# The last two passes of an attention and feed-forward kernel put in order by a planner, and h by w_out in seven block products instead of eight

## The chip, the cores and the metric

The kernel runs on one core of a Trainium2 chip. The metric is the device time of one execution in microseconds; the profile and the trace come from one profiled execution of the same program. In them PE is the matrix engine, PEld its weight loads, DVE the vector engine, ACT the scalar engine, POOL GpSimd and SP the engine that issues most of the DMAs; L1012 is line 1012 of the kernel before.

## The reference

```python
# q, k, v: (8, 8, 576, 64), block-causal attention in blocks of 64
scores = scale * np.matmul(q, k.transpose(0, 1, 3, 2))        # masked where block_i < block_j
attn = np.exp(scores - max);  attn = attn / (sum + 1e-09)
x = np.matmul(attn, v).transpose(0, 2, 1, 3).reshape(4608, 512)
a = x @ w_a            # (512, 1536)
b = x @ w_b            # (512, 1536)
out = (a * b) @ w_out  # (1536, 512)
```

## The kernel before, in words

Every product of the second half is made in float32 quality from three fast products: an operand is cut into a high part (`hi`, a cast by ACT) and a low part (`lo`, what is left, a subtraction by DVE or POOL), and PE adds `hi*hi`, `hi*lo` and `lo*hi`. So one block product of depth 128 is three matmuls.

The 1536 columns of `w_a` and `w_b` are twelve blocks `f` of 128. `f` 0 to 3 are done together with the attention, in the first 598 us: attention and the first feed-forward blocks are a list of operations (`Op`), each with an engine, a cost from the table `TOOK` and a due time (`key`), and `plan()` walks through time and, on the engine that is free first, takes the ready operation with the lowest `key`. The instructions are then issued in that order under `tc.manual_schedule`. The first pass writes its share of the output to a DRAM tensor `part`.

`f` 4 to 7 (`ps_` 0, the second pass) and `f` 8 to 11 (`ps_` 1, the third) are the last passes. Each goes over six pairs of tiles (`tt`, NT2 = 6) of 2 x 384 columns of x. In a pair each `f` is a unit (`pair_unit`): a and b of both tiles come from seven block products instead of eight for each of two depth blocks (`kp`, KP = 2): Y, X1, W1, V1, X2, W2, V2. That is 7 x 2 x 3 = 42 matmuls a unit, L1012, 168 a pair. The operands are sums and differences of blocks of x (`sums_x`, L977 to L993: four subtractions into `xt` and `xr`, four casts into `xh`, four subtractions into `xl` for each `kp`) and of the weights (`sums`). The results need sums too: a unit has four PSUM banks (y, x, w, v). ACT copies y into SBUF (`u`, L1029), DVE adds x (L1030), and five more DVE additions with w, v and u (L1032 to L1039), of which some only wait for the last products W2 and V2, give the factors; two DVE products give `h` of both tiles, and each is cut into hi and lo (`split`, L130 and L133). That makes nine DVE and three ACT instructions a unit. No engine but PE writes a bank.

After the four units `pair_out` makes h by `w_out` for the pair: eight outputs (`j`, `o`), each 4 f x 3 matmuls, 96 a pair, L1058. In the second pass ACT copies each output to `pt` and a GpSimd DMA adds it to `part` (L1122). In the third pass SP loads what `part` holds (L1116), DVE adds (L1124), and SP stores to `outT` (L1125).

The order in the last passes is that of the code, with each engine's queue put in order by the scheduler; `behind_of` holds some DVE instructions back behind others. The weights arrive as float64 and are converted (`convert_w`) by ACT and DVE in the background of these passes: a generator that `background(...)` advances by a step every so many matmuls (`STEP1`, `STEP2`). The second pass's weights are kept in SBUF; those of the third are staged through DRAM (`wabd`, `wod`) and loaded back when the second pass ends. The tiles of x for the next pair (`xr`, L967) are loaded by SP one pair ahead, and `sums_x` for the next pair stands in the code behind unit 2.

Of the kernel before, what the change touches and what calls it, by code (L numbers as in the profile page):

```python
# [17 lines left out]
P = 128  # L18
# [48 lines left out]
STEP1 = 1150  # L67
STEP2 = 2950
# [4 lines left out]
def attention_then_bilinear_ffn(  # L73
# [6 lines left out]

    wo: bass.AP,
    outT: bass.AP,
# [7 lines left out]
    wab, wo = wab.bitcast(I32), wo.bitcast(I32)  # L90
# [14 lines left out]
    part = dram.tile([DO, T], F32, name="part")  # L105
    wabd = dram.tile([F2, KP, P, 2 * NW * P], F32, name="wabd")
    wod = dram.tile([F2, P, 2 * DO], F32, name="wod")
# [80 lines left out]
    wopool = pool(ctx, "wopool", F1)  # L188
# [4 lines left out]

    def new_wo(f):
        w_sb[f][1] = wopool.tile([P, 2, DO], F32R, tag="wo", name=f"wo{f}")
# [21 lines left out]
    def convert_w(todo, lo_eng, paced=False, stage=None, raw=None):  # L217
# [6 lines left out]
        for k, (f, i) in enumerate(todo):  # L224
            now, raw = raw, ahead(*todo[k + 1]) if k + 1 < len(todo) else None
            xf, spare = yield from convert(now, f"w{f}_{i}", paced, own and k == 0)
            if stage:
                st = stage.tile([P, 2, NW if i < KP else NO, P], F32R, tag="st", name=f"st{f}_{i}")
            if i == KP:
                if not stage and w_sb[f][1] is None:  # L230
                    new_wo(f)
                o = st.rearrange("p j c n -> p j (c n)") if stage else w_sb[f][1]
                split(o[:, 0], o[:, 1], xf, nc.scalar, lo_eng)
            elif f < F1:
                ab = w_sb[f][0]
                hi, lo = (ab[:, j, i].rearrange("p c n -> p (c n)") for j in range(2))
                split(hi, lo, xf, nc.scalar, lo_eng)
            else:
                ab = st if stage else w_sb[f][0][:, i]
                yield from sums(ab[:, 0], ab[:, 1], xf, spare, paced)  # L240
            if stage:
                f -= F1 + F2
                nc.sync.dma_start(wod[f] if i == KP else wabd[f, i], f32(st).rearrange("p j c n -> p (j c n)"))
            yield
# [45 lines left out]
    w1 = pool(left, "w1", 1)  # L290
    for f in range(F1):
        w_sb[f] = [w1.tile([P, 2, KP, 4, P], F32R, name=f"wab{f}"), None]
        new_wo(f)
# [68 lines left out]
    def plan():  # L362
# [567 lines left out]
    def start_conv2():  # L930
        raw = fetch(wab[F1, :, 0], f"w{F1}_0")
        box["g"] = convert_w(parts(range(F1, F1 + F2)), nc.vector, paced=True, raw=raw)
# [13 lines left out]
    n_bank = 0  # L946

    def bank(nm):
        nonlocal n_bank
        n_bank += 1  # L950
        return (ps_mm if n_bank % 8 < MM else ps_more).tile([P, 512], F32, tag="mm", name=nm)


    w2 = pool(right, "w2", F2, "right", reuse_waits="tile")
    rpool = pool(right, "rpool", 2 * KP, "right", reuse_waits="tile")
    tpool = pool(right, "tpool", 2, "right", reuse_waits="tile")
    upool = pool(right, "upool", 2, "right", reuse_waits="tile")
# [4 lines left out]
    def load_x(tt):  # L962

        raw = []
        for cc in range(NCC):
            raw.append(rpool.tile([P, 2, T2], F32, tag="xr", name=f"xr{cc}_{tt}"))
            nc.sync.dma_start(  # L967
                raw[cc].rearrange("p j n -> p (j n)"), xd[cc * P:(cc + 1) * P, 2 * tt * T2:2 * (tt + 1) * T2])
        return raw

    def sums_x(raw, kp, nm):

        hi = xk.tile([P, NW, T2], F32R, tag="xh", name=f"xh_{nm}_{kp}", bufs=3)
        t = tpool.tile([P, 3, T2], F32, tag="xt", name=f"xt_{nm}_{kp}")
        a, b = raw[2 * kp:2 * kp + 2]
        v = nc.vector
        for ins in (v.tensor_tensor(t[:, 1], b[:, 1], a[:, 1], op=ALU.subtract),  # L977
                    v.tensor_tensor(a[:, 1], a[:, 1], a[:, 0], op=ALU.subtract)):
            if nm[0] == "0" and nm != "0_0":
                behind_of(ins, "hf")  # L980
        v.tensor_tensor(t[:, 0], b[:, 1], a[:, 1], op=ALU.subtract)
        nc.scalar.copy(hi[:, 0:2], a)
        nc.scalar.copy(hi[:, 2:4], t[:, :2])
        v.tensor_tensor(t[:, 2], b[:, 0], t[:, 0], op=ALU.subtract)
        nc.scalar.copy(hi[:, 4:6], b)
        nc.scalar.copy(hi[:, 6], t[:, 2])
        yield
        lo = xk.tile([P, NW, T2], F32R, tag="xl", name=f"xl_{nm}_{kp}", bufs=2)
        for ins in (
                v.tensor_tensor(lo[:, 0:2], a, f32(hi[:, 0:2]), op=ALU.subtract),  # L990
                v.tensor_tensor(lo[:, 2:4], t[:, :2], f32(hi[:, 2:4]), op=ALU.subtract),
                v.tensor_tensor(lo[:, 4:6], b, f32(hi[:, 4:6]), op=ALU.subtract),
                v.tensor_tensor(lo[:, 6], t[:, 2], f32(hi[:, 6]), op=ALU.subtract)):  # L993
            if nm[0] == "0" and nm != "0_0":
                behind_of(ins, "hf")
        yield hi, lo

    Y, X1, W1, V1, X2, W2, V2 = (4, 2), (0, 0), (3, 1), (5, 3), (1, 4), (6, 5), (2, 6)  # L1000

    def pair_unit(f, xs, nm, hs, halves):

        w = w_sb[f][0]
        y, x, w_, v_ = (bank(f"ps{i}_{nm}")[:, :T2] for i in "yxwv")

        def prod(ps, what, start, kps=range(KP)):
            iw, ix = what
            for kp in kps:
                (xh, xl), wt = xs[kp], w[:, kp]  # L1010
                for i, j in ((0, xh), (0, xl), (1, xh)):
                    nc.tensor.matmul(  # L1012
                        ps, wt[:, i, iw], j[:, ix], start=start and kp == 0 and i == 0 and j is xh,
                        stop=kp == KP - 1 and i == 1, skip_group_check=not start)
                    yield

        if halves:
            for ps, what, kp in ((y, Y, 0), (x, X1, 0), (w_, W1, 0), (y, Y, 1), (x, X1, 1), (v_, V1, 0),
                                 (w_, W1, 1), (v_, V1, 1)):
                yield from prod(ps, what, True, [kp])  # L1020
        else:
            for ps, what in ((y, Y), (x, X1), (w_, W1), (v_, V1)):
                yield from prod(ps, what, True)
        k = (f - F1) % F2
        (ha, la), (hb, lb) = (
            [h_tile(int(4 * k + 2 * j + i >= 10), T2, F32R, f"h{i}_{nm}_{j}") for i in range(2)] for j in range(2))
        u, t, c = (upool.tile([P, T2], F32, tag=f"u{i}", name=f"u{i}_{nm}", bufs=2 - i // 2) for i in range(3))
        v = nc.vector
        nc.scalar.copy(u, y)  # L1029
        v.tensor_tensor(u, x, u, op=ALU.add)  # L1030
# [6 lines left out]
        v.tensor_tensor(t, c, t, op=ALU.mult)  # L1037
        split(hb, lb, t, nc.scalar, nc.vector)
        v.tensor_tensor(u, v_, u, op=ALU.add)  # L1039
        last["hf"] = v.tensor_tensor(u, x, u, op=ALU.mult)  # L1040
        last["la"] = split(ha, la, u, nc.scalar, nc.vector)
        hs[f] = (ha, la), (hb, lb)

    def pair_out(fs, hs, nm, out):

        todo = [(j, o) for j in (1, 0) for o in range(NO)]
        n = {}

        def run(j, o, fs_):
            k = j, o  # L1050
            if k not in n:
                n[k] = 0, bank(f"pso{j}_{o}_{nm}")[:, :T2]
            i, ps = n[k]
            osl = slice(o * P, (o + 1) * P)
            for f in fs_:
                (hh, hl), wt = hs[f][j], w_sb[f][1]
                for a, b in ((0, hh), (0, hl), (1, hh)):
                    nc.tensor.matmul(ps, wt[:, a, osl], b, start=i == 0, stop=i == 3 * len(fs) - 1)  # L1058
                    i += 1
                    yield  # L1060
            n[k] = i, ps
            if i == 3 * len(fs):
                out(j, o, ps)

        for k in todo[:2]:
            yield from run(*k, fs[:-1])
        for k in todo[:2]:
            yield from run(*k, fs[-1:])
        for k in todo[2:]:
            yield from run(*k, fs)  # L1070
# [136 lines left out]
```

## Time and profile before

| what | value |
|---|---|
| median of three runs | 1162.55 us (1158.05 to 1163.65) |
| the profiled execution's own time | 1162.46 us |
| its span in the trace (first to last instruction) | 1160.5 us |
| last passes, first matmul to last | 598.5 us to 1156.9 us |
| matmuls in the last passes | 3168 (12 pairs x 264) |

A page of the profile lists busy time of each engine, the chain of work that ended last, and groups of instructions by line. A row of the windows view gives busy times in a stretch of the span, with the granted clock of PE (1.00 is full speed). In the trace an instruction's duration is printed in microseconds (timeline, chain) or as a mean in nanoseconds (groups). "[1.17 <-DVE u_z]" behind a row says how long its engine stood idle before it and what ended that. Some per cent of the matmul records are missing from the trace, so counts there run a few short.

### The profile page before, as it was taken

How to read it: one execution, taken by the hardware profiler on the slowest of the kernel's cores; microseconds unless marked ns; L12 is line 12 of the kernel's file. 1: busy time of each engine (PE TensorE's matmuls, PEld its weight loads, DVE VectorE, ACT ScalarE, POOL GpSimd, SP SyncE). 2: the span in 40 equal slices, each digit the busy share in tenths (PEclk: the TensorE clock that was granted, in tenths of full speed). 3: DMA queues.
4: the chain of work that ended last, by engine and by line, in shares of the span. 5: the costliest groups of instructions: out<-in, count | busy, mean ns of one | idle time of the engine just before them, and what ended most of it. 6: DMA issues, size and time to landing. Idle time of an engine off the chain costs nothing.

```text
span 1160.5 us, 23135 instructions
## 1 busy us (share of the span) xinstructions
PE 1114.2 (96%) x8400; PEld 1045.4 (90%) x8400; DVE 865.7 (75%) x1813; ACT 539.9 (47%) x1422; POOL 369.5 (32%) x553
## 2 busy tenths in 40 slices
PE   6887989999999999998999999999999999999998
PEld 3566878889988899898999999999999999999998
DVE  5889867778767777752899888797786767767754
ACT  4876556566656656642464453343443221312210
POOL 4686656566656565551100220210201000000000
PEclk8999999999999999998999999999999999999999
DMA  4545787888777777776252662744788415325032
GB/s 160 160 160 150 188 229 225 217 218 219 216 194 211 221 202 223 203 194 177 82 162 73 175 163 81 177 115 126 173 296 225 137 36 156 85 79 163 1 110 69
DMA packets 85554, 187.14 MB, mean 161 GB/s; under 512 B 14272, under 2 KB 40896, under 8 KB 85440
## 3 DMA queue, kind: packets, MB, share of 16 engines
q1 hardware_dynamic: 78528, 176.21, 51.7%
q0 software_dynamic: 6912, 9.44, 5.1%
q8 instruction: 67, 1.10, 0.4%
q14 instruction: 47, 0.39, 0.1%
HBM read 87.03 MB, written 47.19 MB: 116 GB/s over the span
## 4 chain that ended last, share of the span: by engine, by line
PE 74%; DVE 7%; ACT 6%; DMA 5%; SPq 3%; POOL 3%; issue 2%; ACTq 0%; DVEq 0%; POOLq 0%
PE pso_z L1058 16%; PE ps L254 10%; PE psx_z L1012 9%; PE psw_z L1012 9%; PE psv_z L1012 9%; PE pso L254 6%; PE av L660 5%; PE psy_z L1012 4%; PE x L506 3%; ACT e L552 3%; SPq L651 3%; DVE nm L525 2%; PE y L506 2%; DMA qr<-qT 1%; POOL e L595 1%
## 5 line engine op out<-in xcount | busy, mean ns | idle before, releaser
L254 PE MATMUL ps<-xh,wab 128*128 128x288 f32 x1024 | 212.9, 298 | 0.0
L1058 PE MATMUL pso_z<-h_z,wo 128*128 128x384 f32 x1152 | 203.3, 334 | 0.0
L1058 PEld LDWEIGHTS pso_z<-h_z,wo 128*128 128x128 f32 x1152 | 199.9, 188 | 0.4 <-ACT h_z L130 0.3
L254 PEld LDWEIGHTS ps<-xh,wab 128*128 128x128 f32 x1024 | 166.2, 189 | 5.7 <-issue 4.8
L595 POOL TENSOR_SCALAR e<-e,rc 128x512 f32<-128x512 f32 (+3 forms) x256 | 150.6, 607 | 45.3 <-DVE rc L586 45.3
L254 PE MATMUL ps<-xl,wab 128*128 128x288 f32 x512 | 153.9, 301 | 0.6 <-POOL xl L703 0.6
L1122 POOL DMA_DIRECT2D part<-pt x48 | 42.9, 1055 | 283.1 <-ACT pt L1121 275.2
L130 ACT CAST h_z<-u_z 128x384 fp32r<-128x384 f32 x96 | 49.3, 513 | 176.1 <-DVE u_z L1037 160.0
L600 DVE STREAM_TRANSPOSE bl<-e 128x512 f32<-128x512 f32 (+1 forms) x224 | 119.5, 583 | 14.8 <-POOL e L595 10.2
L1012 PE MATMUL psx_z<-xh,wab 128*128 128x384 f32 x384 | 116.0, 338 | 1.2 <-DVE u_z L1030 1.2
L1012 PE MATMUL psv_z<-xh,wab 128*128 128x384 f32 x384 | 116.2, 337 | 0.0
L1012 PE MATMUL psw_z<-xh,wab 128*128 128x384 f32 x384 | 116.1, 338 | 0.0
L660 PE MATMUL av<-at,v 128*64 128x128 f32 (+1 forms) x1920 | 101.3, 264 | 10.4 <-DMA at<-bl 6.4
L660 PEld LDWEIGHTS av<-at,v 128*64 128x64 f32 x1920 | 96.1, 141 | 16.6 <-issue 11.6
L254 PEld LDWEIGHTS ps<-xl,wab 128*128 128x128 f32 x512 | 96.5, 188 | 6.1 <-issue 4.6
L254 PE MATMUL pso<-hh,wo 128*128 128x288 f32 x480 | 101.0, 299 | 0.0
L506 PE MATMUL x<-k,q 64*128 64x512 f32 (+1 forms) x344 | 66.1, 479 | 23.5 <-ACT e L552 17.5
L254 PEld LDWEIGHTS pso<-hh,wo 128*128 128x128 f32 x480 | 78.1, 189 | 5.2 <-issue 4.0
L525 DVE TENSOR_REDUCE nm<-x 128x2 f32<-128x1024 f32 x64 | 73.1, 1142 | 5.7 <-PE x L506 4.7
L760 POOL TENSOR_TENSOR hl<-hf,hh 128x288 fp32r<-128x288 f32 x56 | 46.3, 826 | 97.4 <-ACT hh L756 91.8
L552 ACT ACTIVATE e<-y,nm 128x192 f32<-128x192 f32 (+1 forms) x128 | 62.0, 487 | 26.0 <-DVE nm L525 23.5
L1012 PEld LDWEIGHTS psx_z<-xh,wab 128*128 128x128 f32 x384 | 71.0, 187 | 1.6 <-DVE u_z L1030 1.5
(133 smaller groups left out, 2303.3 us busy)
## 6 DMA issues: line engine op xcount, KB each, us to landing
at<-bl SPq DMA_DIRECT2D x448, 112.0 KB, 2.3
xr<-xd SPq DMA_DIRECT2D x48, 384.0 KB, 4.0
cv<-wab SPq DMA_DIRECT2D x24, 512.0 KB, 4.6
v<-vm SPq DMA_DIRECT2D x32, 320.0 KB, 3.4
xd<-xf SPq DMA_DIRECT2D x32, 288.0 KB, 2.9
part<-ob SPq DMA_DIRECT2D x64, 144.0 KB, 2.1
part<-pt POOLq DMA_DIRECT2D x48, 192.0 KB, 7.0
pt<-part SPq DMA_DIRECT2D x48, 192.0 KB, 3.3
```

The lines of the kernel that those rows point to most:

```text
L130: nc.scalar.copy(hi, src)
L254: nc.tensor.matmul(ps, w_, d_, start=(i == 0), stop=(i == n - 1))
L506: nc.tensor.matmul(out[:, h], qq[r, q0[t]:q0[t] + P], keys, start=j == 0, stop=j == len(qk) - 1)
L525: nc.vector.tensor_reduce(st["nm"][:, :, t], view, axis=AX.X, op=ALU.max, negate=True)
L552: nc.scalar.activation(out, view, AF.Exp, bias=bias, accum_out=sm[:, h, t, :1])
L595: nc.gpsimd.tensor_scalar(ev, ev, st["rc"][:, h, t:t + 1], 1.0, op0=ALU.mult, op1=ALU.mult)
L600: nc.vector.transpose(dst, es[h][t].rearrange("p (c g q) -> p c g q", g=NQ, q=QB))
L660: nc.tensor.matmul(out[d], v[:, h, c], a[:, qs, h, e_], start=start, stop=stop, skip_group_check=True)
L760: nc.gpsimd.tensor_tensor(lo, box2["hf"], f32(hi), op=ALU.subtract)
L1012: nc.tensor.matmul(ps, wt[:, i, iw], j[:, ix], start=start and kp == 0 and i == 0 and j is xh, stop=kp == KP - 1 and i == 1, skip_group_ch ...
L1058: nc.tensor.matmul(ps, wt[:, a, osl], b, start=i == 0, stop=i == 3 * len(fs) - 1)
L1122: nc.gpsimd.dma_start(part[o * P:(o + 1) * P, ts], t, accum_op=ALU.add)
```

## The change

Both last passes become `Op`s as well and go through the planner, with costs for their instructions in `TOOK` (p1 to p4 for 1 to 4 depth blocks on PE, d1, d2 on DVE, a1, a2 on ACT, g1, g2 on POOL, lx for a load of x, acc for an accumulating DMA). The order on PE is that of the code (all products write the name "pe"); for the other engines the planner decides, by due times relative to PE's `clock`. `plan(look)` may now take an operation that becomes ready up to 0.3 us later, if its due time is lower.

A unit now has three banks. W1 and W2 go into the bank of y: ACT copies y to `u`, DVE adds x, and ACT copies the sum back into y's PSUM bank (`middle`, L1100), on which PE then adds W1 (accumulating, not starting) and later W2. Between the two, ACT copies the bank to `t` and DVE adds v (`fourth`). With W2 and V2 the bank holds a factor, and DVE forms `v+u` (`second`). DVE has seven instructions a unit in the second pass instead of nine, ACT five instead of three.

The third pass makes h by `w_out` in seven block products of 8 as well: 28 block products of three matmuls, 84 a pair instead of 96, from sums of blocks of `w_out` (`wq`, four parts, converted and staged like the third pass's `wab`) and differences of h of two units (three more DVE subtractions for every two units, and 14 cuts a pair instead of 8). Its results are made with `middle`, `fourth` and `second` as in a unit. The outputs are added to `outT` by accumulating GpSimd DMAs (`part` is now `outT` itself, so the third pass loads nothing), except in the last pair, where SP loads, DVE adds and SP stores (`finish`); there six `pt` buffers serve eight outputs, and the load for the seventh and eighth is issued behind the store of the first and second.

Of the low parts of x two a pair (`X_POOL`: `kp` 1, groups 0 and 1, 768 columns each) go to POOL instead of DVE. Of the weights for these passes the eight `wab` parts are still converted in the old background; the four parts of `w_out` for f 4 to 7, and all that is staged, are converted by planned operations. Buffers are fixed tiles instead of pools that rotate; `xr` has one set of four.

```diff
-STEP1 = 1150
-STEP2 = 2950
+X_POOL = {(1, 0), (1, 1)}
+BEHIND = 5.0
+LOOK = 0.3
...
-    part = dram.tile([DO, T], F32, name="part")
+    part = outT
...
-            o = min((o for o in ready[e] if since(o) <= t), key=lambda o: (o.key, o.n))
+            o = min((o for o in ready[e] if since(o) <= t + look), key=lambda o: (o.key, o.n))
+            t = max(t, since(o))
...
-        y, x, w_, v_ = (bank(f"ps{i}_{nm}")[:, :T2] for i in "yxwv")
...
-        nc.scalar.copy(u, y)
-        v.tensor_tensor(u, x, u, op=ALU.add)
-        yield from prod(x, X2, False)
-        v.tensor_tensor(t, w_, u, op=ALU.add)
-        yield from prod(w_, W2, False)
-        v.tensor_tensor(t, v_, t, op=ALU.add)
-        yield from prod(v_, V2, False)
-        v.tensor_tensor(c, w_, u, op=ALU.add)
-        v.tensor_tensor(t, c, t, op=ALU.mult)
...
+        def middle(self):
+            self.u = turn_of("u", 4)
+            u, y, x = us[self.u], self.view("y"), self.view("x")
+            name = "u", self.u
+            do("a1", ACT_, lambda: nc.scalar.copy(u, y), [self.name("y")], [name], key=clock[0] - 100)
+            do("d1", DVE_, tt(u, x, u, ALU.add), [self.name("x")], [name], key=clock[0] - 100)
+            do("a1", ACT_, lambda: nc.scalar.copy(y, u), [name], [self.name("y")], key=clock[0] - 100)
+
+        def fourth(self, to, to_name):
+            y = self.view("y")
+            do("a1", ACT_, lambda: nc.scalar.copy(to, y), [self.name("y")], [to_name], key=clock[0] - 100)
+            do("d1", DVE_, tt(to, self.view("v"), to, ALU.add), [self.name("v")], [to_name], key=clock[0] - 100)
...
+        for i in range(F2):
+            if i == 0:
+                units[1].product("Y", ks)
+            units[i].product("X2", ks)
+            units[i].product("W1", ks)
+            fourth(i)
...
+                units[i + 1].middle()
+                units[i + 1].product("V1", ks)
+            else:
+                fill()
+            units[i].product("W2", ks)
+            units[i].product("V2", ks)
+            tail_of(i)
+            if i == 0 and not final:
+                x_load((tt_ + 1) % NT2)
...
+        for z, q in enumerate(outs):
+            q.product("X2", [0])
+            q.product("W1", both_)
+            out(z, q, "fourth")
...
+        do("d1", DVE_, tt(t, src, t, ALU.add), [src_name], [name], key=clock[0] - 50)
+        ts = slice((2 * NT2 - 2 + j) * T2, (2 * NT2 - 1 + j) * T2)
+        do("so", SP_, lambda: nc.sync.dma_start(outT[o * P:(o + 1) * P, ts], t), [name], [], key=clock[0])
+        if z + 6 < len(places):
+            part_load(z + 6)
...
+    for i in range(2 * NT2):
+        tile_pair(*divmod(i, NT2))
+    with tc.manual_schedule(engines={getattr(mybir.EngineType, e) for e in LAGS}):
+        for o in plan(LOOK):
+            o.fn()
```

Where the change moves instructions, the queues of two engines show it. The first place is ACT's queue in units 1 to 3 of a pair of the third pass. Before, ACT has the copy of y (L1029, bank `psy`) and two casts of h (`h0`, L130) for each unit:

```order
L130 CAST h0_z1_4_9_1_13146<-u1_z1_4_9_13149 128x384
L1029 COPY u0_z1_4_10_13225<-psy_z1_4_10_13193 128x384
L130 CAST h0_z1_4_9_0_13144<-u0_z1_4_9_13148 128x384
L130 CAST h0_z1_4_10_1_13223<-u1_z1_4_10_13226 128x384
L1029 COPY u0_z1_4_11_13300<-psy_z1_4_11_13268 128x384
```

Now it has, for each unit, the copy of the bank (L1098), the copy back into it (L1100), the copy for `fourth` (L1104), and more casts of h (`hz`, L1113), with a cast of the next x between them (L1008):

```order
L1113 CAST hz8_0_8536<-u3_8519 128x384
L1104 COPY t0_8520<-bank0_8508 128x384
L1098 COPY u1_8517<-bank3_8511 128x384
L1100 COPY bank3_8511<-u1_8517 128x384
L1008 CAST xh2_8402<-xt1_7883 128x768
L1113 CAST hz2_1_8540<-u3_8519 128x384
L1113 CAST hz4_1_8542<-u0_8516 128x384
L1104 COPY t1_8521<-bank3_8511 128x384
```

What moved: a bank is now read, written and read again by ACT within a unit, with W1 of PE between the last two.

The second place is DVE's queue where one pair of the third pass ends and the next begins. Before, the last additions to `part` (L1124, `pt`) are followed directly by the sums of the next pair's first unit:

```order
L1124 TENSOR_TENSOR pt0_1_4_1_13191<-pso0_1_z1_4_13432,pt0_1_4_1_13191 128x384
L1124 TENSOR_TENSOR pt0_2_4_1_13378<-pso0_2_z1_4_13447,pt0_2_4_1_13378 128x384
L1124 TENSOR_TENSOR pt0_3_4_1_13385<-pso0_3_z1_4_13462,pt0_3_4_1_13385 128x384
L1030 TENSOR_TENSOR u0_z1_5_8_13509<-psx_z1_5_8_13478,u0_z1_5_8_13509 128x384
L1032 TENSOR_TENSOR u1_z1_5_8_13510<-psw_z1_5_8_13479,u0_z1_5_8_13509 128x384
L1034 TENSOR_TENSOR u1_z1_5_8_13510<-psv_z1_5_8_13480,u1_z1_5_8_13510 128x384
```

Now the last low parts of this pair boundary's x (`xl1`, L1013) stand ahead of the first sums for the pair after the next one (`xt`, `xr`, L978, from the loads of x into `xr0` to `xr3`), and these ahead of the next pair's `middle` (`u2<-bank7,u2`):

```order
L1013 TENSOR_TENSOR xl1_8404<-xr3_7881,xh1_8401 128x768
L1013 TENSOR_TENSOR xl1_8404<-xt1_7883,xh1_8401 128x384
L978 TENSOR_TENSOR pt3_8525<-bank2_8510,u0_8516 128x384
L978 TENSOR_TENSOR xt0_7882<-xr1_7879,xr0_7878 128x384
L978 TENSOR_TENSOR xr0_7878<-xr0_7878 128x384
L978 TENSOR_TENSOR xt0_7882<-xr1_7879,xr0_7878 128x384
L978 TENSOR_TENSOR xt0_7882<-xr1_7879,xt0_7882 128x384
L978 TENSOR_TENSOR xt1_7883<-xr3_7881,xr2_7880 128x384
L978 TENSOR_TENSOR xr2_7880<-xr2_7880 128x384
L978 TENSOR_TENSOR u2_8518<-bank7_8515,u2_8518 128x384
```

What moved: the first subtractions on newly loaded x stand at the start of a pair, ahead of its first unit's sum; before, they stood behind unit 2. `xr3` can be loaded anew when its low part (the first row above) has been taken.

More of the change, by code (lines that the diff above doesn't have):

```diff
@@ L89, in attention_then_bilinear_ffn @@
     NCC = DO // P
-    wab, wo = wab.bitcast(I32), wo.bitcast(I32)
+    wab, wo, wq = wab.bitcast(I32), wo.bitcast(I32), wq.bitcast(I32)
     NO = DO // P
@@ L971, in sums_x @@
[L971 to L996, printed above, removed]
@@ L1044, in pair_out @@
[L1044 to L1070, printed above, removed]
+    xr = [rpool.tile([P, 2, T2], F32, tag=f"xr{cc}", name=f"xr{cc}") for cc in range(NCC)]
@@ new lines, in attention_then_bilinear_ffn, with turn_of, products, go @@
+    st = stage.tile([P, 2, NW, P], F32R, tag="st", name="st")
+    count = dict.fromkeys(("bank", "u", "t", "pt", "conv"), 0)
+    def turn_of(what, n):
+        count[what] += 1
+        return (count[what] - 1) % n
+    def products(bk, terms, n, start, names):
+        def go():
+            i = 0
+            for (wh, wl), (dh, dl) in terms():
+                for a, b in ((wh, dh), (wh, dl), (wl, dh)):
+                    nc.tensor.matmul(banks[bk], a, b, start=start and not i, stop=i == 3 * n - 1, skip_group_check=not start)
+                    i += 1
+        o = do(f"p{n}", PE_, go, names, [("bank", bk), "pe"], key=clock[0])
+        clock[0] += o.took
+        return o
@@ new lines, in attention_then_bilinear_ffn, with __init__, product, view @@
+    Y, X1, W1, V1, X2, W2, V2 = (4, 2), (0, 0), (3, 1), (5, 3), (1, 4), (6, 5), (2, 6)
+    class Unit:
+        def __init__(self, terms):
+            self.terms = terms
+            self.bk = {}
+            self.begun = set()
+        def product(self, what, ks):
+            b, w, d = {"Y": ("y", *Y), "X1": ("x", *X1), "V1": ("v", *V1), "X2": ("x", *X2), "W1": ("y", *W1),
+                       "W2": ("y", *W2), "V2": ("v", *V2)}[what]
+            if b not in self.bk:
+                self.bk[b] = turn_of("bank", 8)
+            names = [x for k in ks for x in self.terms(k, w, d)[1]]
+            products(self.bk[b], lambda: [self.terms(k, w, d)[0]() for k in ks], len(ks), b not in self.begun, names)
+            self.begun.add(b)
+        def view(self, b):
+            return banks[self.bk[b]]
+        def name(self, b):
+            return "bank", self.bk[b]
+        def middle(self):
[9 more added lines that the diff above has]
+            do("d1", DVE_, tt(to, self.view("v"), to, ALU.add), [self.name("v")], [to_name], key=clock[0] - 100)
+        def second(self, to, to_name):
+            do("d1", DVE_, tt(to, self.view("v"), us[self.u], ALU.add), [self.name("v"), ("u", self.u)], [to_name],
+               key=clock[0] - 50)
@@ new lines, in attention_then_bilinear_ffn, with evacuate, copy_of @@
+    wq_sb = {}
+    def evacuate(o, j, tt_, make):
+        i = turn_of("pt", 6)
+        t, name = pts[i], ("pt", i)
+        make(t, name)
+        ts = slice((2 * tt_ + j) * T2, (2 * tt_ + j + 1) * T2)
+        do("acc", POOL_, lambda: nc.gpsimd.dma_start(part[o * P:(o + 1) * P, ts], t, accum_op=ALU.add), [name],
+           [("part", o, 2 * tt_ + j)], key=clock[0] - 60)
+    def copy_of(unit, b):
+        return lambda t, name: do("a1", ACT_, lambda: nc.scalar.copy(t, unit.view(b)), [unit.name(b)], [name], key=clock[0] - 50)
```

456 lines of the change are left out of this document (324 added, 132 removed), and 4 rows, old and new, of the table TOOK.

## The prediction

> **What bounds the kernel now.** The page comes first: PE is busy 96% of the span and holds most of the chain that ended last.
>
> ```profile
> span 1160.5 us, 23135 instructions
> PE 1114.2 (96%) x8400; PEld 1045.4 (90%) x8400; DVE 865.7 (75%) x1813; ACT 539.9 (47%) x1422; POOL 369.5 (32%) x553
> PE 74%; DVE 7%; ACT 6%; DMA 5%; SPq 3%; POOL 3%; issue 2%; ACTq 0%; DVEq 0%; POOLq 0%
> ```
>
> The windows of the second pass, of the third, and of one pair in the third show that nothing is left there but matmuls:
>
> ```profile
> 598.50:877.70 279.20, 278.04 (x1586) 276.77 (x1585) 235.77 (x464) 119.28 (x217) 42.02 (x47) 1.00 0.57 159
> 877.70:1156.90 279.20, 277.92 (x1586) 277.28 (x1584) 186.43 (x343) 62.97 (x111) 0.86 (x1) 1.00 0.35 102
> 971.20:1017.50 46.30, 46.30 (x266) 46.30 (x265) 33.22 (x62) 11.69 (x20) 0.00 (x0) 1.00 0.34 97
> ```
>
> PE is busy for all but 2.4 of 558.4 us, at a granted clock of 1.00, and the waits of PE add up to the same:
>
> ```profile
> PE psx_z L1012 <- DVE u_z L1030: 1.2, 1, 1.2
> PE psy_z L1012 <- DVE xl L991: 0.7, 1, 0.7
> PE psy_z L1012 <- ACT xh L983: 0.5, 1, 0.5
> ```
>
> The other engines have room: in the third pass DVE is busy 186.4 of 279.2 us, ACT 63. So the last passes cost what their matmuls cost, and a change can gain by fewer matmuls, by a shorter distance between them, and by those 2.4 us. The chain of one pair gives the distance, first in the w_a and w_b products, then in h by w_out:
>
> ```profile
> 975.75 1.06 PE psx_z L1012 x6
> 1001.19 16.64 PE pso_z L1058 x96
> ```
>
> 1.06/6 = 176.7 ns and 16.64/96 = 173.3 ns. A pair is 168 x 176.7 + 96 x 173.3 = 29.69 + 16.64 = 46.32 us; the window has 46.30.
>
> **The change: matmuls.** The second pass keeps 6 pairs of 46.32, 277.9 us. A pair of the third has 84 instead of 96 matmuls behind the units: 29.69 + 84 x 173.3 = 44.24, six of them 265.4. Together 543.3 against 558.4: at most 15.1 us are to be had, 12.5 by 72 matmuls, the rest by waits and unevenness that go. The rows put W1 and W2 on a bank that ACT wrote; I take no price for that on PE itself, since the operands and their sizes are the same. The `wq` products might run at 176.7 as the wab ones do: 504 x 3.4 ns = 1.7 us; I take 0.6, as h by w_out is the nearer row.
>
> **The copy back.** Its hops are in the trace, around the wait of 1.17 us:
>
> ```profile
> 882.19 0.48 ACT L1029 COPY u_z<-psy_z 128x384 f32<-128x384 f32 x1
> 882.71 0.56 DVE L1030 TENSOR_TENSOR u_z<-psx_z,u_z 128x384 f32<-128x384 f32 x1
> 883.32 0.45 PE L1012 MATMUL psx_z<-xh,wab 128*128 128x384 f32 x1 [1.17 <-DVE u_z L1030]
> ```
>
> and the casts and low parts that can stand before them in groups of one third-pass pair:
>
> ```profile
> L130 ACT CAST h_z<-u_z 128x384 fp32r<-128x384 f32 x8 | 4.1, 513 | 16.4 <-DVE u_z L1037 15.5 <-DVE u_z L1040 0.5
> L990 DVE TENSOR_TENSOR xl<-xr,xh 128x768 fp32r<-128x768 f32 x2 | 1.9, 948 | 0.0
> L982 ACT CAST xh<-xr 128x768 fp32r<-128x768 f32 x2 | 1.7, 836 | 7.8 <-PE psv_z L1012 4.6 <-DVE xr L978 3.2
> ```
>
> ACT copy to PE is 1.13 us; X2 needs the first two. W1 needs one more ACT copy, 0.52 with its handover: 1.65. Behind the products that `middle` reads PE has 9 matmuls before X2 in unit 0 (1.59 us) and 15 before W1 (2.65), in the other units 18 (3.2). So it is free where ACT and DVE come at once, and their due time (100 ahead) puts them first in the queue; if a cast of x (0.84) stands before it, unit 0 has 0.2 to 0.5 us left. A copy writing PSUM beside PE is not in this trace: I take it to last as long as the copy that reads it, 0.48; the nearest margin is unit 0's, 1.0 us before W1, so even at double length nothing waits; no gain is possible from it. In the third pass the fill is 6 matmuls, 1.06 us, against one copy, 0.52.
>
> **The first pair.** DVE works off weights there, at these durations:
>
> ```profile
> L181 DVE SCALAR_TENSOR_TENSOR cv<-cv 128x512 int32<-128x512 int32 x5 | 3.4, 687 | 0.0
> L133 DVE TENSOR_TENSOR wo<-cv,wo 128x512 fp32r<-128x512 f32 x4 | 2.7, 684 | 0.0
> L173 DVE TENSOR_SCALAR cv<-cv 128x512 int32<-128x512 int32 x6 | 2.5, 420 | 0.0
> L1030 DVE TENSOR_TENSOR u_z<-psx_z,u_z 128x384 f32<-128x384 f32 x4 | 2.2, 550 | 0.0
> L208 DVE TENSOR_TENSOR cv<-cv 128x128 f32<-128x128 f32 x4 | 1.0, 288 | 0.0
> ```
>
> The planned order fills PE's gap behind unit 3 with the first output's products with f 4, 5 and 6, which needs the third part of w_out and unit 2's last low part. In DVE's queue these come behind a rest of the last wab part (2 x 0.42 + 3 x 0.69 + 4 x 0.29 + 0.55 + 0.68 = 5.3), some three and a half parts of w_out (2 x 0.42 + 4 x 0.69 = 3.6 each) and 22 instructions of 0.55: 30 us. PE comes there after 156 matmuls, 27.6. The difference is 2.4; instructions that follow each other overlap by some 0.08, which takes 2 to 3 away, and waits for PE, ACT and loads add some. I take 1.5, from 0 to 3.
>
> **Subtractions on POOL.** Nothing of 768 columns ran on POOL. The nearest rows are
>
> ```profile
> L703 POOL TENSOR_TENSOR xl<-xf,xh 128x288 fp32r<-128x288 f32 x62 | 51.3, 838 | 15.3 <-ACT xh L699 15.3
> L490 POOL TENSOR_TENSOR k<-kr,k 128x576 fp32r<-128x576 f32 x22 | 31.6, 1437 | 40.2 <-ACT k L486 37.6 <-ACT xf L678 1.4 <-issue 1.1
> L482 DVE SCALAR_TENSOR_TENSOR q<-qr,q x22: 825/970/1606, 157.0 to 491.9; 128x640 fp32r<-128x640 f32 x22
> ```
>
> From 288 to 576 columns it grows by 0.60, so 768 take 1.8 us (an estimate). DVE gains 0.95 twice a pair, which no wait asks for. The price is beside it: the last row's DVE instruction, alone 0.83, took up to 1.61 in the stretch in which POOL subtracts, 0.78 more. Both POOL subtractions of a pair fall where unit 3's tail leads to the second half of h by w_out. That chain is a product, two subtractions, a cast and a low part, 4 x 0.55 + 0.51, with handovers about 3.2 us, against 21 matmuls, 3.68: 0.46 left. A slowing of 0.5 to 0.8 leaves 0 to 0.3 of wait a pair, one of up to 1.8 leaves 1.3. I take 0.5, 3.0 for six pairs, with 0 and 8 as ends. [...]
>
> **The end.** The last matmul ends where DVE's last addition begins:
>
> ```profile
> 1144.41 0.86 SPq L1125 DMA_DIRECT2D outT<-pt  x2
> 1156.83 0.56 DVE L1124 TENSOR_TENSOR pt<-pso_z,pt 128x384 f32<-128x384 f32 x1 [1.53 <-PE pso_z L1058]
> pt<-part SPq DMA_DIRECT2D x48, 192.0 KB, 3.3
> outT<-pt SPq DMA_DIRECT2D x48, 192.0 KB, 3.7
> ```
>
> From 1156.9 to 1160.5 are 3.6 us. Now two DVE additions stand there instead of one, +0.55. The loads for the seventh and eighth output wait for the stores of the first and second: 3.6 and 0.3 of issue from the bank to the store's end and 3.3 for the load make some 7.2 behind the second W1, against 30 matmuls and an addition, 6.1: 1.1 late. Together 1.6, from 0.55 to 2.7.
>
> **The sum.** 277.9 + 265.4 + 0.6 + 1.5 + 3.0 = 548.4; 598.5 + 548.4 = 1146.9; with 3.6 + 1.6 the span is 1152.1. The profiled execution took 1162.46, 1.96 above its span and 0.1 under the median, so the time is 1154.1, rounded 1154.
>
> **Rivals.**
>
> *PE at the shorter distance.* For some 40 us the same wab products ran closer together:
>
> ```profile
> 651.20 1.04 PE psx_z L1012 x6
> ```
>
> That is 173.3 ns. I know no cause; it came directly after PE had waited. If the new order keeps it, twelve pairs gain 168 x 3.4 ns = 0.57 each, 6.8: 1147. Against it: it held for one pair in twelve.
>
> *POOL holds DVE.* As above with 8 instead of 3, and the same in the second pass where tails are tight, say 2: 1161, no change. For it: the 0.78. [...]
>
> *x comes late, and it ends slower.* At the boundary in the third pass DVE's queue has `xt1<-xr3` ahead of the next pair's `middle`. `xr3` is free some 13.8 us after the last W1 of unit 3 (66 matmuls, 11.5, then a copy, an addition and a low part of 0.95). With 0.3 of issue, a landing L and two subtractions of 0.47 it must be done by 111 matmuls and a copy, 19.75. So L may be 4.7 us.
>
> ```profile
> DMA to landing us min/median/max: 3.1/4.0/6.9
> part<-pt POOLq DMA_DIRECT2D x48, 192.0 KB, 7.0
> ```
>
> At the median nothing is lost. Each pair loses L - 4.7, and from L = 6.1 on six pairs lose the 8.4 that were gained; at 6.9 they lose 13, 1167, and at 7.5 17, 1171. For it: the accumulating DMAs, now in the third pass too, take 7.0 to land. Against it: the 4.0 holds beside such DMAs in the second pass.
>
> *The products are not fewer on the chip*: 3096 follow from the order, so this has no chance.
>
> **How the numbers follow.** The forecast 0.68, the shorter distance 0.10, POOL 0.15, late x 0.07. Own range of the forecast: without waits and with the small ends 1148, with 3 at the start, 6 for POOL, 1.7 for wq and 2.7 at the end 1160. The range runs from 1147 to 1161: it takes in the shorter distance and most of the POOL case, and leaves out late x and the upper half of POOL, some 0.15 with the edges. A measurement can tell 0.5% from no change, 5.8 us: faster is under 1156.7, slower over 1168.4. Faster: 0.10 and four fifths of 0.68, with a little of POOL at half force, 0.68; slower, late x from L = 7.1 on, 0.05; the same, the rest, 0.27.
>
> **What would show it.** Right: pairs of 44.2 to 44.8 in the third pass's windows, 46.3 in the second's, PE waits of under 8 us in all, the biggest at the first pair's fill and at Y of the second half. POOL: `xl1` on POOL near 1.8 us, DVE instructions beside it far above 0.56, PE waiting for `hy` low parts. Late x: PE waits for a copy back behind `xt1<-xr3`, with DVE idle for DMA `xr`. Wrong altogether would be waits of PE in every unit for the copy back into the bank, or a distance over 177 ns on banks that ACT wrote.

## The result, and the profile after

The changed kernel takes 1178.5 us (median; 1176.8 to 1180.7) beside 1160.3 us of the kernel before on the same chip: 1.0158 times as long, interval 1.0119 to 1.0197. The forecast was 1154, its range 1147 to 1161. The change made the kernel slower, by 1.6%. One execution of one of the kernels below, `both`, fell in a far slower state (1341.1 us) and counts in no ratio.

The page of the profile after shows fewer matmuls (8328, 72 less) and PE less busy, with POOL up from 32% to 38%:

```profile
span 1176.5 us, 23057 instructions
PE 1110.5 (94%) x8328; PEld 1033.3 (88%) x8328; DVE 880.5 (75%) x1795; ACT 624.8 (53%) x1614; POOL 446.2 (38%) x615
PE 62%; DVE 16%; DMA 8%; ACT 6%; issue 3%; SPq 2%; POOL 2%; DVEq 0%; ACTq 0%; POOLq 0%
```

PE now holds 62% of the chain that ended last instead of 74%, DVE 16 instead of 7, DMA 8 instead of 5. The windows of the second pass, the third, and one of its pairs (start:end, length, busy time of PE, PEld, DVE, ACT and POOL, PE's clock, DMA share, GB/s):

```profile
596.40:888.80 292.40, 282.15 (x1586) 279.34 (x1585) 231.09 (x431) 142.57 (x271) 63.80 (x59) 0.99 0.58 162
888.80:1170.30 281.50, 270.70 (x1514) 263.15 (x1512) 206.49 (x355) 124.80 (x249) 57.30 (x52) 1.00 0.35 72
983.10:1030.50 47.40, 45.15 (x253) 43.61 (x252) 36.55 (x63) 22.24 (x45) 11.25 (x11) 1.00 0.36 67
```

The second pass took 292.4 instead of 279.2 us, the third 281.5 instead of 279.2, though each of its pairs has 12 matmuls less. PE stood still for 10 to 11 us in each. Its waits name the releasers (us in total, times, the longest). Line numbers are now those of the changed kernel: L1061 is every product of the last passes, L978 the helper that issues most of DVE's sums and products, L1104 the copy in `fourth`; `hz` and `hy` are the two sets of buffers for parts of h:

```profile
PE bank L1061 <- DVE u L978: 10.3, 7, 4.2
PE bank L1061 <- ACT t L1104: 4.8, 5, 1.0
PE bank L1061 <- DVE hz L1114: 2.5, 3, 1.5
PE bank L1061 <- ACT hy L1113: 1.4, 5, 0.3
PE bank L1061 <- DVE t L978: 1.3, 6, 0.2
```

20.9 us with a last small row, against 2.4 before. A delay that is given below without a row is taken from the starts of two matmuls, their distance less the usual 0.17; it is some 0.17 longer than the idle time in a row. Two chains of events stand behind the waits.

**A DVE subtraction stands still beside POOL's.** The timelines of POOL, DVE, ACT and PE in the third pass, where unit 3's `fourth` stands (start, duration, engine, line, and what ended the idle time before):

```profile
960.72 2.23 POOL L1013 TENSOR_TENSOR xl<-xt,xh 128x768 fp32r<-128x768 f32 x1 [18.32 <-PE bank L1061]
961.15 2.22 DVE L1114 TENSOR_TENSOR hz<-u,hz 128x384 fp32r<-128x384 f32 x1
963.76 1.14 DVE L978 TENSOR_TENSOR u<-bank,u 128x384 f32<-128x384 f32 x2
964.93 0.51 ACT L1113 CAST hz<-u 128x384 fp32r<-128x384 f32 x1 [3.93 <-DVE u L978]
965.35 0.47 ACT L1104 COPY t<-bank 128x384 f32<-128x384 f32 x1
965.87 0.44 PE L1061 MATMUL bank<-xh,wab 128*128 128x384 f32 x1 [0.99 <-ACT t L1104]
```

DVE's low part `hz` normally takes 0.55. Here it takes 2.22 and ends 0.42 after POOL's subtraction. So `u` is late, ACT's cast of `u` is late, and behind that cast in ACT's queue stands the copy `t<-bank`. PE may not put W2 on that bank before the copy has read it. The page's releaser, ACT, is the last link; the first is POOL. Six microseconds later the same happens to a low part of x (2.62, 0.95 elsewhere), and the chain to the second half of h by w_out is 1.3 us late in three pieces:

```profile
966.68 2.01 POOL L1013 TENSOR_TENSOR xl<-xr,xh 128x768 fp32r<-128x768 f32 x1 [3.73 <-PE bank L1061]
966.88 2.62 DVE L1013 TENSOR_TENSOR xl<-xr,xh 128x768 fp32r<-128x768 f32 x1
```

A DVE instruction that reads a PSUM bank as one of its operands keeps its 0.56, although it runs wholly beside POOL's (all twelve such instructions of the last passes took 0.55 to 0.56):

```profile
725.76 1.85 POOL L1013 TENSOR_TENSOR xl<-xt,xh 128x768 fp32r<-128x768 f32 x1 [25.71 <-PE bank L1061]
725.79 0.56 DVE L978 TENSOR_TENSOR t<-bank,t 128x384 f32<-128x384 f32 x1
```

A DVE instruction with a single operand (`cv`, in SBUF), 0.42 elsewhere, stands as well: it takes 1.62 and ends 0.28 after POOL's:

```profile
675.06 1.86 POOL L1013 TENSOR_TENSOR xl<-xt,xh 128x768 fp32r<-128x768 f32 x1 [24.30 <-ACT xh L1008]
675.58 1.62 DVE L1135 TENSOR_SCALAR cv<-cv 128x512 int32<-128x512 int32 x1
```

**x lands late.** The boundary of two pairs in the third pass, SP, DVE, ACT and PE:

```profile
980.09 0.32 SPq L983 DMA_DIRECT2D xr<-xd  x1
986.36 0.56 DVE L978 TENSOR_TENSOR xt<-xr,xr 128x384 f32<-128x384 f32 x1 [2.36 <-DMA xr<-xd]
987.50 0.55 DVE L978 TENSOR_TENSOR u<-bank,u 128x384 f32<-128x384 f32 x1
988.11 0.45 PE L1061 MATMUL bank<-xh,wab 128*128 128x384 f32 x1 [0.62 <-DVE u L978]
```

`xr3` is issued at 980.09 and used at 986.36, 6.3 us later; the planner had counted on 4.0 behind 0.5 of issue. DVE stands 2.36 us in front of `xt<-xr,xr` with the first unit's sum behind it in its queue, and PE waits for that sum. At the start of the second pair of the second pass both come together (POOL's part is the smaller there: without it, in no_pool below, PE still waits 3.59 us):

```profile
642.24 2.62 POOL L1013 TENSOR_TENSOR xl<-xt,xh 128x768 fp32r<-128x768 f32 x1
642.48 2.80 DVE L1013 TENSOR_TENSOR xl<-xt,xh 128x384 fp32r<-128x384 f32 x1
650.56 0.56 DVE L978 TENSOR_TENSOR xt<-xr,xr 128x384 f32<-128x384 f32 x1 [1.02 <-DMA xr<-xd]
653.42 0.69 PE L1061 MATMUL bank<-xh,wab 128*128 128x384 f32 x1 [4.24 <-DVE u L978]
```

### The profile page after: what moved, and what is told of

Same layout as the page of the kernel before. It is cut to its first block, busy times and chain, and to the rows that moved or that the text cites. A ratio compares the mean times of both kernels' runs of the same rounds, so it can differ in the third digit from the quotient of the medians.

```text
span 1176.5 us, 23057 instructions
## 1 busy us (share of the span) xinstructions
PE 1110.5 (94%) x8328; PEld 1033.3 (88%) x8328; DVE 880.5 (75%) x1795; ACT 624.8 (53%) x1614; POOL 446.2 (38%) x615
## 4 chain that ended last, share of the span: by engine, by line
PE 62%; DVE 16%; DMA 8%; ACT 6%; issue 3%; SPq 2%; POOL 2%; DVEq 0%; ACTq 0%; POOLq 0%
PE bank L1061 32%; PE ps L249 11%; PE pso L249 7%; PE av L656 5%; PE x L502 3%; ACT e L548 3%; DMA xr<-xd 3%; DVE xl L1013 2%; DVE nm L521 2%; PE y L502 2%; DVE u L978 2%; DVE hz L1114 2%; SPq L647 2%; DMA qr<-qT 1%; DVE bl L596 1%
## 5 line engine op out<-in xcount | busy, mean ns | idle before, releaser
L1061 PE MATMUL bank<-xh,wab 128*128 128x384 f32 x1344 | 353.2, 340 | 15.2 <-DVE u L978 10.3
L1061 PEld LDWEIGHTS bank<-xh,wab 128*128 128x128 f32 x1344 | 246.2, 189 | 19.7 <-DVE u L978 12.5
L1061 PE MATMUL bank<-xl,wab 128*128 128x384 f32 x672 | 227.6, 339 | 0.0
L1167 POOL DMA_DIRECT2D outT<-pt x88 | 77.5, 1132 | 208.7 <-ACT pt L1325 139.1
L1061 PEld LDWEIGHTS bank<-xl,wab 128*128 128x128 f32 x672 | 127.0, 189 | 0.0
L978 DVE TENSOR_TENSOR u<-bank,u 128x384 f32<-128x384 f32 x158 | 87.7, 555 | 37.1 <-PE bank L1061 32.9
L1061 PE MATMUL bank<-hz,wo 128*128 128x384 f32 x612 | 111.2, 335 | 2.5 <-DVE hz L1114 2.5
L1061 PEld LDWEIGHTS bank<-hz,wo 128*128 128x128 f32 x612 | 106.4, 188 | 3.8 <-DVE hz L1114 3.8
L1013 POOL TENSOR_TENSOR xl<-xt,xh 128x768 fp32r<-128x768 f32 x11 | 23.1, 2096 | 213.7 <-ACT xh L1008 109.1
L978 DVE TENSOR_TENSOR t<-bank,t 128x384 f32<-128x384 f32 x98 | 54.4, 555 | 56.6 <-PE bank L1061 28.0
```

Of the source, the lines that this page charges most:

```text
L978: return lambda: v.tensor_tensor(o, a, b, op=op)
L1013: lambda h_=h_, l_=l_, src=src, eng_=eng_: eng_.tensor_tensor(l_, src, f32(h_), op=ALU.subtract),
L1061: nc.tensor.matmul(banks[bk], a, b, start=start and not i, stop=i == 3 * n - 1, skip_group_check=not start)
L1167: do("acc", POOL_, lambda: nc.gpsimd.dma_start(part[o * P:(o + 1) * P, ts], t, accum_op=ALU.add), [name], [("part", o, 2 * tt_ + j)], key= ...
```

## The experiments

The theory from this trace: POOL's subtractions and late transfers each cost 10 to 15 us, and the rest of the change does what the forecast said. Rivals: only one of the two is a cause and the other is cover; or the copy into a bank, or the planned order, has a price of its own. The table gives every run: the median, the ratio to the kernel before with its 95% interval, and from one profiled execution the second pass, the third pass, and the time from the last matmul's start to the end of the span. What stands ahead of the last passes took 592 to 600 us in these executions, and the changed kernels do not differ in it, so the last column adds only the other three. The runs were made on several chips, each beside the kernel before, so small differences are to be read from the last column or the ratios.

| kernel | median us | ratio to before | pass 2 | pass 3 | end | sum |
|---|---|---|---|---|---|---|
| before | 1158.4 to 1160.3 | 1 | 279.2 | 278.7 | 4.0 | 562.0 |
| after | 1178.5 | 1.0158 (1.0119 to 1.0197) | 292.4 | 281.3 | 6.3 | 580.1 |
| no_pool | 1163.2 | 1.0028 (1.0009 to 1.0047) | 284.9 | 272.8 | 6.3 | 564.0 |
| late_dma | 1172.0 | 1.0096 (1.0061 to 1.0131) | 287.6 | 278.6 | 6.2 | 572.4 |
| both | 1152.2 | 0.9921 (0.9894 to 0.9949) | 284.1 | 265.3 | 6.3 | 555.6 |
| before_pool | 1184.1 | 1.0204 (1.0171 to 1.0238) | 287.5 | 293.4 | 4.3 | 585.2 |
| both_x | 1147.2 | 0.9894 (0.9858 to 0.9930) | 280.0 | 265.3 | 6.2 | 551.4 |
| pool_halves | 1162.6 | 1.0020 (0.9996 to 1.0043) | 287.4 | 272.0 | 6.6 | 566.0 |
| best | 1150.8 | 0.9917 (0.9886 to 0.9948) | 283.1 | 265.3 | 4.6 | 552.9 |
| best_x | 1147.5 | 0.9907 (0.9873 to 0.9941) | 279.6 | 265.3 | 4.6 | 549.4 |

**POOL's part taken away**

```diff
-X_POOL = {(1, 0), (1, 1)}
+X_POOL = set()
```

> The changed kernel with X_POOL empty: all low parts of x on DVE, nothing else edited. Theory POOL (a DVE subtraction of two SBUF operands stands still for the whole of a POOL subtraction, and what stands behind it is late): the waits of PE before W2 of unit 3 (1.05 to 1.15 us) and before the second half of h by w_out (0.40 + 0.44 + 0.42) go from five pairs of the third pass, 2.4 x 5 = 12 us, and 2 to 4 us in the second pass; 1178.5 becomes 1162 to 1166. No DVE instruction of 384 columns is longer than 0.6 us in the last passes. Rival transfers (DVE stands before the sum of the first unit because x or a staged store is late): the POOL waits were only cover, the time stays within 3 us of 1178.5, since DVE gets 2 x 0.95 us a pair more to do. Rival copy-back (W1, W2 on a bank that ACT wrote cost by themselves): no change either.

1163.2 us, as the POOL theory has it: 16.0 us less from the first matmul of the last passes to the end, though DVE has 1.9 us more to do in each pair. The waits before W2 and in h by w_out are gone from all five pairs. The split was not as expected: the second pass gained 7.5 us instead of 2 to 4, the third 8.5 instead of 12. What stays is the other cause, larger in the third pass than with POOL's part (why was not tried): DVE waits for `xr` at four boundaries of the third pass, here 4.23 us, and PE is 0.8 to 2.2 us late.

```profile
976.02 0.56 DVE L978 TENSOR_TENSOR xt<-xr,xr 128x384 f32<-128x384 f32 x1 [4.23 <-DMA xr<-xd]
976.50 0.55 DVE L978 TENSOR_TENSOR u<-bank,u 128x384 f32<-128x384 f32 x1
```

**Transfers given more time in the plan**

```diff
-    "lx": (0.5, 4.0, 0), "lw": (0.5, 4.6, 0), "sw": (0.5, 3.0, 0),
+    "lx": (0.5, 8.0, 0), "lw": (0.5, 8.0, 0), "sw": (0.5, 7.0, 0),
```

(The entries stand in two lines of the table.) Nothing but the order changes: in DVE's queue `u2<-bank7,u2` moves ahead of `xt1<-xr3`.

> The changed kernel with three landing times in the planner's table raised: lx 4.0 to 8.0, lw 4.6 to 8.0, sw 3.0 to 7.0; the instructions are the same, only the order differs: at a pair's start DVE's queue has the first unit's sum ahead of the subtractions that wait for x. Theory transfers: PE's waits before X2 or W1 of unit 0 go (0.73 to 0.95 us in five pairs of the third pass, and 4.4, 2.0 and 1.6 us with some 2.5 us of slow matmuls behind them in the second): 12 to 14 us, 1164 to 1167. Theory POOL alone: those waits come from DVE held by POOL and stay; under 3 us change. Both theories together: 1164 to 1167 as well, with the 1.1 + 1.3 us of waits in each pair of the third pass left as they are.

1172.0 us, 6 to 7 less than the change (7.7 in the last column), half of what was expected. In the third pass it is as expected: the wait at unit 0 is gone from every pair, the 1.06 us before W2 and the three pieces in h by w_out stay, and a pair takes 46.9. In the second pass only 4.8 us are gained; the first pair became longer, 52.7 us instead of 48.4. That pair waits for w_out, which comes later by the larger `lw`, as both_x shows below.

**Both**

> The changed kernel with X_POOL empty and the three landing times raised. If POOL and transfers are the two causes and add up: 1178.5 - 14 - 13 = 1151 to 1154, faster than the kernel before (1160), with PE waits of under 6 us in the last passes and pairs of 44.3 to 45 us in the third pass. If the copy back into the bank or the planned order has a price of its own, PE waits stay at unit 0's or every unit's W1 and the time stays above 1160.

1152.2 us, within the expected 1151 to 1154, and faster than the kernel before by 0.8%. All pairs of the third pass take 44.24 us, the forecast's number, and those of the second 46.32 but the first. In the last passes PE waits twice, both times in the first pair, and its granted clock is 0.51 for 5.5 us behind these waits, which costs that pair another 2.4 us:

```profile
PE bank L1061 <- DVE hz L1114: 1.7, 1, 1.7
PE bank L1061 <- ACT wo L1143: 1.4, 1, 1.4
```

So beyond the first pair neither the copy into a bank nor the planned order has a price of its own. And the two causes are not cover for each other: in the last column POOL's part is worth 16.0 us with the old landing times and 16.7 with the new, the new landing times 7.7 with POOL's part and 8.4 without it.

**POOL's part alone, in the kernel before**

```diff
-                v.tensor_tensor(lo[:, 0:2], a, f32(hi[:, 0:2]), op=ALU.subtract),
-                v.tensor_tensor(lo[:, 2:4], t[:, :2], f32(hi[:, 2:4]), op=ALU.subtract),
+                (nc.gpsimd if kp else v).tensor_tensor(lo[:, 0:2], a, f32(hi[:, 0:2]), op=ALU.subtract),
+                (nc.gpsimd if kp else v).tensor_tensor(lo[:, 2:4], t[:, :2], f32(hi[:, 2:4]), op=ALU.subtract),
```

> The kernel before with only the two subtractions (kp 1, groups 0 and 1) of each pair moved from DVE to POOL. Theory POOL: DVE subtractions beside them are stretched to 2 us and more, those that read a PSUM bank stay at 0.56; since DVE has a third of its time free in the third pass, PE waits only where the low parts themselves or the last unit's h are late, 0 to 1 us a pair: 1160 to 1170. If POOL harmed nothing by itself (only by the planned order): DVE instructions at their old durations, 1158 to 1161.

1184.1 us, 24 more than before: the mechanism was right, the size, at most 10, far too small. The two subtractions moved to POOL cost the old kernel more than the whole change did. Timelines of POOL, DVE and PE in its third pass:

```profile
917.74 2.12 POOL L990 TENSOR_TENSOR xl<-xr,xh 128x768 fp32r<-128x768 f32 x1 [25.93 <-DVE xl L990]
918.51 2.16 DVE L991 TENSOR_TENSOR xl<-xt,xh 128x768 fp32r<-128x768 f32 x1
919.82 2.51 POOL L991 TENSOR_TENSOR xl<-xt,xh 128x768 fp32r<-128x768 f32 x1
920.59 2.15 DVE L133 TENSOR_TENSOR h_z<-u_z,h_z 128x384 fp32r<-128x384 f32 x1
922.67 0.55 DVE L1040 TENSOR_TENSOR u_z<-psx_z,u_z 128x384 f32<-128x384 f32 x1
922.80 0.44 PE L1058 MATMUL pso_z<-h_z,wo 128*128 128x384 f32 x1 [2.25 <-DVE h_z L133]
```

DVE and POOL take turns: `xl` on DVE (2.16, 0.95 elsewhere), `xl` on POOL (2.51), `h_z` on DVE (2.15, 0.55 elsewhere), and each ends behind the other engine's, by 0.81, 1.66 and 0.41. `h_z` is the one that PE waits for, 2.25 us at a time, once in each of five pairs behind the last unit. That DVE had a third of its time free did not help. But this is half of the 23.2 us by which the last column grows; most of the rest is a second effect, in the second pass, where PE waits for low parts that POOL itself makes, and about 5 us are lost at half clock behind three of the waits:

```profile
PE pso_z L1058 <- DVE h_z L133: 11.2, 5, 2.3
PE psy_z L1012 <- POOL xl L991: 6.6, 2, 4.5
```

**POOL's subtractions in halves**, on the kernel late_dma:

```diff
+                if pool_:
+                    for z in range(2):
+                        add("g1", POOL_, lambda h_=h_[:, z], l_=l_[:, z], src=src[:, z]: nc.gpsimd.tensor_tensor(
+                            l_, src, f32(h_), op=ALU.subtract), ...
```

> The three landing times raised and X_POOL as in the change, but each POOL subtraction of 768 columns made as two of 384, the same work on POOL. [...] If POOL slows DVE by its traffic and not by instruction, the sum of the slowing is the same and the time stays at 1170 to 1174.

1162.6 us against 1172.0 (6.4 less in the last column), and not the 1170 to 1174 of a slowing by traffic. Pairs of the third pass take 45.6 instead of 46.9. DVE's two instructions, 2.22 and 2.62 in the change (2.23 and 2.62 in late_dma), take 1.38 and 1.78; each ends 0.88 ahead of the end of the second half (POOL's two rows are pairs of instructions):

```profile
903.84 2.68 POOL L1014 TENSOR_TENSOR xl<-xt,xh 128x384 fp32r<-128x384 f32 x2 [21.21 <-issue]
904.26 1.38 DVE L1120 TENSOR_TENSOR hz<-u,hz 128x384 fp32r<-128x384 f32 x1
908.95 2.86 POOL L1014 TENSOR_TENSOR xl<-xr,xh 128x384 fp32r<-128x384 f32 x2 [2.43 <-PE bank L1067]
909.15 1.78 DVE L1019 TENSOR_TENSOR xl<-xr,xh 128x768 fp32r<-128x768 f32 x1
```

POOL works on the same data and DVE's two instructions are 0.84 shorter each. So what DVE stands here goes by the length of one POOL instruction (2.23 and 2.01 whole, 2.68 and 2.86 for two halves), not by the data that POOL works on.

**Only x given more time** (X_POOL empty, `lx` 8.0, `lw` and `sw` as in the change)

> X_POOL empty and only the landing time of x raised (lx 4.0 to 8.0; lw and sw as in the change). If the late transfers are those of x alone: within 2 us of the kernel with all three raised (1152). If the staged stores of weights matter too (DVE's subtraction into st stands ahead of the first unit's sum in the second pass): 2 to 5 us above it, 1154 to 1157, with PE waits of 1 to 4 us at the start of pairs 2 to 5.

1147.2 us, 5 below both (4.2 in the last column), where I expected the same within 2 us, or more. The first pair takes 48.4 instead of 52.5, the rest is the same to 0.1 us. So in the second pass too x was what came late, and the larger `lw` only made the planner put the four parts of w_out later in DVE's queue than PE needs them: the third part is finished 30.3 us behind the first matmul in both and 27.9 in both_x, and PE comes for it after some 28. (`sw` was put back too, but the first store that it plans comes 58 us behind the first matmul.) PE waits once:

```profile
PE bank L1061 <- DVE hz L1114: 1.5, 1, 1.5
```

The windows of the second pass, the third, and one pair:

```profile
593.70:873.70 280.00, 278.52 (x1587) 277.88 (x1586) 230.86 (x443) 143.35 (x271) 40.57 (x47) 1.00 0.60 169
873.70:1139.10 265.40, 265.40 (x1513) 265.24 (x1511) 197.49 (x365) 125.93 (x249) 36.85 (x42) 1.00 0.37 77
962.10:1006.40 44.30, 44.30 (x255) 44.30 (x254) 34.76 (x64) 22.52 (x44) 7.13 (x9) 1.00 0.37 73
```

PE has no gap in the whole third pass.

**The last loads**, on both (best) and on both_x (best_x): the seventh and eighth part go into `xr`, which the last pair does not need.

```diff
+        if z < 6:
+            i = turn_of("pt", 6)
+            to, names = pts[i], [("pt", i)]
+        else:
+            to, names = xr[z - 6][:, 0], [("xr", z - 6, 0)]
...
-        if z + 6 < len(places):
-            part_load(z + 6)
```

> X_POOL empty, three landing times raised, and in the last pair the seventh and eighth part of the output are loaded at once into xr, which is free there, rather than into pt behind the stores. The wait of the last addition for its load (1.35 us in the changed kernel) goes: 1150 to 1151 against 1152. If the end is set by the store alone: no change.

> X_POOL empty, only the landing time of x raised, and the last two loads of the last pair into xr. From the first matmul of the last passes to the end of the span the kernel with X_POOL empty and lx raised took 551.4 us, the change of the last loads took 1.7 us off the end: 549.7, and with a first part of 594 to 598 us a time of 1145.5 to 1149.5, faster than before by 1%. If the gain of the smaller first pair (48.4 instead of 52.5 us) was chance and not the order, 1150 to 1152.

The last addition of the change, and of best_x:

```profile
1172.88 0.56 DVE L978 TENSOR_TENSOR pt<-u,pt 128x384 f32<-128x384 f32 x1 [1.35 <-DMA pt<-outT]
```

```profile
1141.30 0.56 DVE L978 TENSOR_TENSOR xr<-u,xr 128x384 f32<-128x384 f32 x1
```

The wait for the load is gone and the end is 4.6 us long instead of 6.2 to 6.3. In the medians 1.3 us (both to best, as expected) and nothing (both_x to best_x, 1147.2 and 1147.5) are seen of it, less than the intervals can tell; the stretch itself is from the traces. best_x has the shortest sum of all, 549.4 us against 562.0, and is 0.9% faster than the kernel before.

## Why the prediction was wrong

**What bounds the kernel** was right: PE, and a gap in it counts. both_x, with one wait of 1.5 us, has 545.3 us in the two passes for matmuls forecast at 543.3; the change, with 20.9 of waits, has 573.7.

**Matmuls**: right. 44.24 us a pair and 265.4 for the pass were forecast; both_x has 44.24 and 265.4. The 0.6 us for `wq` at a larger distance was not needed, and the shorter distance (173.3 ns throughout) did not come.

**The copy back**: right. PE waits for the copy into the bank (L1100) in none of these kernels, the change included. The wait for `u` in the change is one step earlier, X2 waiting for the sum that stands behind `xr` in DVE's queue.

**The first pair**: right. 1.5 us were forecast for the fill behind unit 3; PE waits 1.5 to 1.7 for `hz` there in all of the kernels with the planned order; those with the larger `lw` wait another 1.4 for `wo`.

**Subtractions on POOL**: this step failed. It put the term at 0.5 us of wait a pair, from a DVE row that was lengthened by 0.78, and called a slowing of 1.8 the far end. The change has 2.35 us a pair in the third pass (1.15 before W2, 0.40 + 0.44 + 0.42 in h by w_out), 12 us in five pairs, and some in the second. From after to no_pool the price is 16.0 us, from late_dma to both 16.7, against 3.0 forecast and 8 as its end. The 0.78 was not the size of the slowing: in the kernel before, that DVE instruction (L482, 438.40 to 440.01) began 0.93 before the end of a POOL subtraction of 1.46 (L490, 437.87 to 439.33), so 0.78 was most of what was left of POOL's. The rows of the change go the same way: 2.22 and 2.62 beside POOL's 2.23 and 2.01, 0.56 where one operand is a bank; in pool_halves 1.38, where POOL's instruction is half as long. I had named a slowing of up to 1.8 and weighed it too low. For the chain to the second half of h by w_out the working was good: at full length it gave 1.3 a pair, and 0.40 + 0.44 + 0.42 were measured. But I looked at that chain only. The other, by way of ACT's queue to the copy that W2 waits for, I had called covered by 6 matmuls.

**Late x**: the rival was named, with its place, and got 0.07. Its working held roughly: a landing of up to 4.7 us behind 0.3 of issue is free. What failed was the landing: the median over all four loads of a pair, 4.0, stood for the last of them, which is the one that counts. In the change it took 6.1 to 6.3 from the start of its issue, at four boundaries of the third pass, where the first loads of the same pairs took 3.1 to 3.7. At 6.3 the working gives 1.3 us a pair in six pairs; the change has 0.7 to 1.0 in four, no_pool 0.8 to 2.2 in four. The reason against the rival, that 4.0 holds beside accumulating DMAs in the second pass, fails on the trace before itself: the last load of a pair took 4.2 to 6.6 there, and 4.1 to 4.5 in the third pass, which issues one such DMA, at its start. That these DMAs are what makes it late was not tried. With the second pass late x is worth 12.6 us (no_pool to both_x).

**The rivals as a set**: I gave the two cases separate chances as if one excluded the other. They add up, as the four kernels after, no_pool, late_dma and both show. Without the two, both_x has 551.4 us from the first matmul of the last passes to the end; the forecast without its 3.0 for POOL was 550.6, so the rest of the sum was right to 1 us. 562.0 - 551.4 = 10.6 is what the change gains without them; forecast were 8.4.

**The end**: 1.6 us more than before were forecast, 2.3 measured, with the wait for the last load (1.35) as the main part, as forecast.

## What to carry to other kernels

Before work goes to POOL to relieve DVE, ask which DVE instructions will run beside it: those that read no bank and began while it ran stood here until it ended (2.22 us instead of 0.55 beside 2.23 on POOL), and a third of DVE's time free did not pay for that when one of them was on PE's path (24 us more in before_pool). A planner's cost for a transfer decides what stands in front of what in an engine's queue; take the time of the last transfer of a group (6.1 to 6.3 us here), not the median of all (4.0 in the kernel before), and put what PE waits for ahead of what a DMA may hold. In a stretch without a gap fewer matmuls became time one to one (12 of 173.3 ns less, 44.24 instead of 46.32 us a pair), with gaps they did not (47.4 in the change); so look for each new gap along every queue that leads to PE, the copies of ACT included.

## What the runs showed of the hardware that was not expected

After some waits PE ran at about half clock, in the change for 3.4 us behind each of two. Behind the wait of 4.24 us, the granted clock (the eighth number) is

```profile
653.40:656.80 3.40, 3.38 (x11) 3.38 (x12) 2.71 (x7) 1.92 (x4) 0.00 (x0) 0.52 0.00 0
656.80:660.00 3.20, 3.20 (x20) 3.20 (x19) 2.17 (x5) 1.50 (x3) 0.00 (x0) 1.00 0.92 286
```

Matmuls came some 315 ns apart instead of 175, and the wait cost 1.6 us more than its length. The same followed a wait of 1.81 us (0.55 over 704.2 to 708.0), and one of 1.89 in no_pool (0.58 over 977.0 to 980.5), but not one of 2.04 there (1.00). Of the five waits of 2.25 us in before_pool two were followed by it and three were not; the stretches behind the first and the third:

```profile
922.80:926.20 3.40, 3.40 (x19) 3.40 (x20) 3.40 (x6) 1.25 (x2) 0.00 (x0) 1.00 0.31 71
1021.30:1024.70 3.40, 3.40 (x13) 3.40 (x12) 3.40 (x7) 0.91 (x2) 0.00 (x0) 0.50 0.42 117
```

So the length of the wait alone does not decide; what does was not tried.
